# Attention and two mixture layers on one core: the third block's bias is begun later in the second block

## The chip, the core and the metric

The kernel runs on one core of a Trainium2 chip. The metric is the device time of one execution in microseconds (us); lower is better. The engines are TensorE (PE: matmuls; PEld: its weight loads), VectorE (DVE), ScalarE (ACT), GpSimd (POOL) and SyncE (SP, which here issues nearly all DMAs, in order).

## What is computed

Attention over 4 batches, 8 heads, 576 positions and head size 64, with a learned bias on relative position, and then two feed-forward layers over the 2304 rows:

```python
scores = scale * np.matmul(q, k.transpose(0, 1, 3, 2))
x = (psi_rel / psi_i)[..., None]            # log1p(|i-j|) / log1p(max(i,1))
bias = np.maximum(x @ w1 + b1, 0.0) @ w2    # 576 x 576 x 8 heads
attn = softmax(scores + bias)               # bias is the same for all batches
x = (attn @ v) as 2304 x 512
h = np.maximum(np.maximum(x @ w1, x @ w2), x @ w3)   # 512 -> 768
x = h @ w_out                                        # 768 -> 512
h = x @ w_in                                         # 512 -> 2048
x = g(h) @ w_out                                     # g: 0, a parabola, or h
```

## The kernel before

The 576 query positions are cut into five blocks: four of 128 and one of 64. The work on attention is a list of slots, each one head of one batch of one block: slots 0 to 31 are the first block, 32 to 63 the second, 64 to 95 the third, and then the fourth and the short fifth, interleaved. A slot has these steps:

- scores on TensorE (L692), made for two slots at a time into two PSUM buffers of the tile `s`;
- the softmax step on VectorE (L706): scores plus bias, and the row's extreme, which frees the buffer of `s`;
- the exponential (L708) and a cast to 16 bits (L724) on ScalarE, the residue of the cast on GpSimd (L725, a first part, and L726);
- a transpose by DMA on SP's queue (L728) into the tile `pt`;
- 14 value matmuls (L748), called for three slots later.

After the last slot of a batch the result is scaled (L760, VectorE), cast (L762) and its residue made (L763), and transposed by DMA into `xT` (L771).

Between these steps the kernel's slot loop puts other work:

- The bias of the next block, 18 groups for a block of 128. A group is a mask on VectorE (L390), 16 short matmuls on TensorE (L394), and a sum that every other group does on VectorE (L400, L401), the others on ScalarE and GpSimd (L403 to L406). The sum reads `xtab`, a table that is loaded from memory for each block (L298) and scaled on VectorE (L308); there is one buffer of it. Bias of two blocks is held at a time, in the two halves of `ab`; that of the short block lies in `ws` (L374 to L381, nine groups, its own table by L303).
- The first feed-forward layer for blocks that are done. Its first part is 12 matmuls of L803 for each of three weights, in one of three PSUM buffers of the tile `pm`. The first of a triple is emptied by ScalarE (L808), the others by VectorE (L810), and the maximum is cast (L814) and its residue made by GpSimd (L815). Its second part is 18 matmuls of L825, emptied by ScalarE (L830), reduced by VectorE (L831) and stored (L832).
- The split of the second part's weights into two 16-bit parts: six times L158 on ScalarE and L159 on VectorE, from slot 38 on.

How much of the bias a slot calls for is set by one list, a pair for each of the first three blocks: from which slot of the block on, and over how many slots. The loop adds a rate at every slot from the first number on, and calls for a group whenever the sum passes a whole number:

```python
b_at, b_n = PRM["bias"][min(u.j, 2)]
with sooner("bias"):
    for _ in range(rate("bias", (27 if u.j == 2 else 18) / b_n) if at >= b_at and not conv_left else 0):
        if bias_q:
```

The calls do not fix the final order. A scheduler orders the instructions of each engine by the priority of their calls (`sooner` lifts it) and by its own estimate of when inputs are ready. Each engine then runs its list in order.

Of the kernel before, what the change touches and what calls it, by code (L numbers as in the profile page):

```python
# [20 lines left out]
def kernel(ctx: ExitStack, tc: tile.TileContext, qt, kt, vr, small, mw1, mw2, mw3, mwo, win, wo2, out):  # L21
# [30 lines left out]
        peng='vv',  # L52
        warm=50,
        warm1=30,
        bias=[[12, 10], [6, 16], [3, 26]],
        c0=0.7,
        conv=[0.9, 0.36, 0.36, 0.36, 0.36],
        mlp=[2, 1.2, 1.5, 1.2, 1],
# [1193 lines left out]
```

## Time and profile before

| | |
|---|---|
| timed runs | median 1025.28 us of 3 (1022.13 to 1028.06) |
| profiled execution | 1021.94 us, its span 1020.2 us |
| TensorE busy | 937.5 us (92%) |
| VectorE, ScalarE, GpSimd busy | 716.9, 599.4, 512.1 us |
| mean granted clock of TensorE | 0.954 of full |

The span is the time between the first and the last instruction of the profiled execution. Busy times are sums over an engine's instructions; matmuls are pipelined, so a busy TensorE is not one at its peak. In the rows below, the number in square brackets behind an instruction is how long its engine stood idle before it and what ended that.

### The profile page before, as it was taken

How to read it: one execution, taken by the hardware profiler on the slowest of the kernel's cores; microseconds unless marked ns; L12 is line 12 of the kernel's file. 1: busy time of each engine (PE TensorE's matmuls, PEld its weight loads, DVE VectorE, ACT ScalarE, POOL GpSimd, SP SyncE). 2: the span in 40 equal slices, each digit the busy share in tenths (PEclk: the TensorE clock that was granted, in tenths of full speed). 3: DMA queues.
4: the chain of work that ended last, by engine and by line, in shares of the span. 5: the costliest groups of instructions: out<-in, count | busy, mean ns of one | idle time of the engine just before them, and what ended most of it. 6: DMA issues, size and time to landing. Idle time of an engine off the chain costs nothing. (4 is left out here: it accounts for less than half of the span.)

```text
span 1020.2 us, 26008 instructions
## 1 busy us (share of the span) xinstructions
PE 937.5 (92%) x10258; PEld 761.2 (75%) x10258; DVE 716.9 (70%) x1603; ACT 599.4 (59%) x1194; POOL 512.1 (50%) x734
## 2 busy tenths in 40 slices
PE   5768889899999989999999899979999999999996
PEld 5546678668888878777778778434588888888885
DVE  8897977796456677555454588798687686586565
ACT  3688875865556544769576689443344354444342
POOL 4132577676576754646357102886034344444452
PEclk7777879999999999999999999999999999999999
DMA  9897988999798988999999754010020010000000
GB/s 281 260 282 147 256 208 205 217 220 227 144 249 192 185 188 183 222 220 232 217 177 210 181 191 127 21 42 1 1 84 22 2 42 12 12 22 11 12 22 21
DMA packets 238970, 141.47 MB, mean 139 GB/s; under 512 B 187520, under 2 KB 217728, under 8 KB 238336
## 3 DMA queue, kind: packets, MB, share of 16 engines
q1 hardware_dynamic: 238688, 139.55, 58.5%
q8 instruction: 80, 1.31, 0.5%
q14 instruction: 42, 0.34, 0.1%
q10 hardware_dynamic: 160, 0.26, 0.1%
HBM read 79.68 MB, written 15.27 MB: 93 GB/s over the span
## 5 line engine op out<-in xcount | busy, mean ns | idle before, releaser
L803 PEld LDWEIGHTS <-aw 128*128 128x128 f16 x2160 | 190.6, 99 | 44.0 <-issue 22.0
L803 PE MATMUL pm<-xT,aw 128*128 128x256 f16 (+1 forms) x1812 | 203.9, 265 | 4.8 <-ACT hm L808 1.9
L726 POOL TENSOR_TENSOR phl<-sp,phl 128x512 f16<-128x512 f32 x136 | 160.9, 1183 | 0.0
L708 ACT ACTIVATE sp<-sp,mx 128x576 f32<-128x576 f32 x144 | 110.6, 768 | 77.6 <-DVE mx L706 77.2
L692 PE MATMUL s<-k,qz 64*128 64x288 f32 (+1 forms) x576 | 130.4, 464 | 11.6 <-DVE mx L706 9.0
L725 POOL TENSOR_TENSOR phl<-sp,phl 128x64 f16<-128x64 f32 x136 | 50.1, 368 | 176.0 <-ACT phl L724 143.0
L706 DVE CUSTOM_DVE_ANT_0 sp<-s,ab 128x576 f32<-128x576 f32 x128 | 93.2, 751 | 30.0 <-PE s L692 11.8
L1137 ACT ACTIVATE sp<-pm,vec 128x256 f32<-128x256 f32 x112 | 61.3, 556 | 85.9 <-PE pm L1120 84.6
L748 PEld LDWEIGHTS <-pt 128*128 128x128 f16 x1792 | 73.1, 101 | 30.2 <-DMA pt<-phl 20.1
L692 PEld LDWEIGHTS s<-k,qz 64*128 64x128 f32 (+1 forms) x576 | 70.8, 203 | 30.9 <-DVE mx L706 11.0
L724 ACT ACTIVATE phl<-sp 128x576 f16<-128x576 f32 x136 | 89.7, 673 | 3.6 <-DMA pt<-phl 3.0
L1141 POOL TENSOR_TENSOR hh<-hh 128x128 f32<-128x128 f32 x56 | 34.4, 614 | 107.9 <-DVE hh L1139 92.1
L748 PE MATMUL pav<-v,pt 128*128 128x64 f16 x1568 | 70.5, 196 | 14.6 <-DMA pt<-phl 14.5
L1120 PEld LDWEIGHTS <-ab 128*128 128x128 f16 x756 | 73.9, 98 | 9.4
L1138 DVE SCALAR_TENSOR_TENSOR hh<-pm,vec,sp 128x256 f32<-128x256 f32 x112 | 52.2, 477 | 33.5 <-ACT sp L1137 33.2
L825 PEld LDWEIGHTS <-wo 128*128 128x128 f16 x648 | 62.4, 99 | 15.9 <-issue 6.1
L825 PE MATMUL pm<-hh,wo 128*128 128x256 f16 x558 | 69.1, 276 | 3.6 <-ACT hh L814 1.4
L815 POOL TENSOR_TENSOR hh<-hm,hh 128x256 f16<-128x256 f32 (+1 forms) x60 | 44.0, 733 | 56.7 <-ACT hh L814 55.4
L1159 PEld LDWEIGHTS <-xT 128*128 128x128 f16 x588 | 57.5, 98 | 7.8 <-ACT xT L1146 1.2
L1159 PEld LDWEIGHTS <-wo 128*128 128x128 f16 x588 | 57.5, 98 | 6.7
L810 DVE SCALAR_TENSOR_TENSOR hm<-pm,hm 128x256 f32<-128x256 f32 (+1 forms) x108 | 41.9, 389 | 28.1 <-ACT hm L808 12.2
L1142 POOL TENSOR_TENSOR hh<-hh 128x128 f32<-128x128 f32 x56 | 26.5, 473 | 68.0 <-DVE hh L1139 61.0
(300 smaller groups left out, 2024.8 us busy)
## 6 DMA issues: line engine op xcount, KB each, us to landing
k<-in_k_dram SPq DMA_DIRECT2D x64, 288.0 KB, 4.0
v<-v_d SPq DMA_DIRECT2D x24, 640.0 KB, 4.9
ws<-in_moe_w_out_dram SPq DMA_DIRECT2D x15, 512.0 KB, 4.9
ws<-in_moe_w_in_dram SPq DMA_DIRECT2D x9, 512.0 KB, 5.1
x_d<-hl SPq DMA_DIRECT2D x36, 128.0 KB, 2.7
qz<-in_q_dram SPq DMA_DIRECT2D x16, 256.0 KB, 4.6
ab<-in_moe_w_dram SPq DMA_DIRECT2D x8, 512.0 KB, 9.3
qz<-x_d SPq DMA_DIRECT2D x4, 1024.0 KB, 4.7
```

The source lines that it names most:

```text
L692: last_score[0] = T.matmul(sbox[i + r][:, c, :288], q[p, s if u.j == SJ else s // 2], k[p, 288 * c:288 * c + 288], start=True, stop=True)
L706: last_pair[0] = V.tensor_tensor_reduce(halves(sn), sbox.pop(i)[:, :, :288], halves(bias_sb[u.j][:, h]), -0.125, 3e38, ALU.add, ALU.min, mx)
L708: last_soft[0] = A.activation(pf, sn, AF.Exp, scale=-1.0, bias=mx, accum_out=u.sums[:, h:h + 1])
L724: A.activation(hl[:, :S], pf, AF.Copy)
L726: G.tensor_tensor(hl[:, S + 64:], pf[:, :512], hl[:, :512], ALU.subtract)
L748: T.matmul(u.pav[:, 64 * h:64 * h + 64], pt[:, c], v[:, sl, 64 * (h % 4):64 * (h % 4) + 64], **kw)
L803: T.matmul(o, wm[:, ft, i, wp, kk], x_rhs(key, xp, kk) if n == 256 else x_rhs(key, xp, kk)[:, c], start=(x == 0), stop=(x == 11))
L825: T.matmul(pm, wo16[:, ft, wp, P * d:P * d + P], hh[:, ft, hp], start=(ft == 0 and y == 0), stop=(ft == NF1 - 1 and y == 2))
L1120: T.matmul(pm, w[:, wp, kk], x2t[ORDER[y]][:, kk, xp, 256 * sub:256 * sub + 256], start=(x == 0), stop=(x == 11))
L1137: A.activation(r, pm, AF.Relu, scale=c_ch[:, f], bias=c_half)
L1138: V.scalar_tensor_tensor(t, pm, c_c[:, f], r, ALU.mult, ALU.max)
L1159: T.matmul(m[x], gl[:, gp, i], w[:, wp], start=(start and z == 0 and x % 2 == 0), stop=(stop and z == 2 and (x % 2 == 1 or x == 6)))
```

## The change

The list's second pair is changed. The third block's bias is called for from the twelfth slot of the second block on (slot 44), not from the sixth (slot 38); the rate stays 18 groups in 16 slots.

```diff
         warm=50,
         warm1=30,
-        bias=[[12, 10], [6, 16], [3, 26]],
+        bias=[[12, 10], [12, 16], [3, 26]],
         c0=0.7,
```

The numbers of instructions stay as they are. The order of the engines differs between about slot 44 and slot 60, and in small ways between slots 84 and 92, where the short block's bias is built. On TensorE, before, the 18 runs of L394 stand between the scores of slots 44 and 58, after, between those of slots 46 and 60. Between the scores of slots 44 and 46 TensorE now has 72 matmuls of L803 where it had 36 and two runs of L394, and ahead of the value matmuls of slot 42 it has 60 of L803 and 18 of L825 more than before and one run of L394 less; the second part (L825) of the first layer's second unit begins ahead of the scores of slot 48, where it began behind those of slot 50. By the scores of slot 60 all has been done that had been done before.

VectorE, from slot 45 to slot 47; `wo` are the second part's weights, `ab` the bias, `hm` the first part's results. Before:

```order
L400 TENSOR_TENSOR btmp<-pm,xtab 128x256
L390 TENSOR_TENSOR masks<-rw,thr 128x1024
L401 SCALAR_TENSOR_TENSOR ab<-pm,vec,btmp 128x8x32
L810 SCALAR_TENSOR_TENSOR hm<-pm,hm 128x256
L159 SCALAR_TENSOR_TENSOR wo<-ws,vec,wo 128x512
L390 TENSOR_TENSOR masks<-rw,thr 128x1024
L159 SCALAR_TENSOR_TENSOR wo<-ws,vec,wo 128x512
L760 TENSOR_TENSOR xf<-pav,rd 128x512
L159 SCALAR_TENSOR_TENSOR wo<-ws,vec,wo 128x512 x2
L706 ISA sp,mx<-s,ab 128x576
```

And after, on VectorE at the same place:

```order
L810 SCALAR_TENSOR_TENSOR hm<-pm,hm 128x256
L159 SCALAR_TENSOR_TENSOR wo<-ws,vec,wo 128x512 x6
L760 TENSOR_TENSOR xf<-pav,rd 128x512
L810 SCALAR_TENSOR_TENSOR hm<-pm,hm 128x256 x2
L706 ISA sp,mx<-s,ab 128x576
L706 ISA mx 128x1
L706 ISA sp,mx<-s,ab 128x576
L706 ISA mx 128x1
L757 TENSOR_SCALAR rd<-sums 128x8
L758 RECIPROCAL rd<-rd 128x8
L810 SCALAR_TENSOR_TENSOR hm<-pm,hm 128x256 x2
```

The masks and sums of the bias have gone from among the six splits, two emptyings of the first part stand directly behind them, and the softmax steps of slots 46 and 47 follow each other.

ScalarE at the same place, after the change; `phl` are the 16-bit parts of a slot's exponentials, `hh` those of the first part's results:

```order
L158 ACTIVATE wo<-ws,vec 128x512 x6
L724 ACTIVATE phl<-sp 128x576
L814 ACTIVATE hh<-hm 128x256
L808 ACTIVATE hm<-pm 128x256
L762 ACTIVATE px<-xf 128x512
L814 ACTIVATE hh<-hm 128x256
L708 ACTIVATE sp,sums<-sp,mx 128x576 x2
L808 ACTIVATE hm<-pm 128x256
L724 ACTIVATE phl<-sp 128x576 x2
L814 ACTIVATE hh<-hm 128x256
```

Before, the two operations of the bias (L403, L404) stood behind the first cast here, and the exponentials of slots 46 and 47 were apart, with casts between them.

VectorE at the reload of `xtab` for the fourth block. Before, ahead of the softmax step of slot 58:

```order
L390 TENSOR_TENSOR masks<-rw,thr 128x1024
L810 SCALAR_TENSOR_TENSOR hm<-pm,hm 128x256
L308 TENSOR_SCALAR xtab<-xtab,vec 128x576
L810 SCALAR_TENSOR_TENSOR hm<-pm,hm 128x256
L706 ISA sp,mx<-s,ab 128x576
```

And after, on VectorE, where the steps around it are those of slots 60 and 61:

```order
L390 TENSOR_TENSOR masks<-rw,thr 128x1024
L760 TENSOR_TENSOR xf<-pav,rd 128x512
L706 ISA sp,mx<-s,ab 128x576
L706 ISA mx 128x1
L308 TENSOR_SCALAR xtab<-xtab,vec 128x576
L706 ISA sp,mx<-s,ab 128x576
L706 ISA mx 128x1
L810 SCALAR_TENSOR_TENSOR hm<-pm,hm 128x256 x2
```

The scaling of the reloaded table has moved from ahead of slot 58 to between the softmax steps of slots 60 and 61.

## Rows read from the trace of the kernel before

**Rows 1.** The page: TensorE's busy time, and the chain's shares by engine.

```profile
PE 937.5 (92%) x10258; PEld 761.2 (75%) x10258; DVE 716.9 (70%) x1603; ACT 599.4 (59%) x1194; POOL 512.1 (50%) x734
...
PE 30%; DVE 5%; DMA 3%; ACT 3%; POOL 2%; issue 1%; SPq 0%; POOLq 0%; ACTq 0%; DVEq 0%
```

**Rows 2.** Stretches: us from:to, length, busy us by engine (instructions), clock, DMA, GB/s.

```profile
210.00:220.00 10.00, 8.43 (x91) 6.42 (x92) 10.00 (x20) 5.51 (x12) 9.15 (x12) 0.83 1.16 212
200.00:270.00 70.00, 65.30 (x888) 53.45 (x886) 50.68 (x101) 39.91 (x95) 46.74 (x58) 0.98 0.98 204
270.00:360.00 90.00, 89.93 (x1265) 77.22 (x1263) 53.64 (x128) 55.20 (x136) 63.51 (x84) 1.00 0.99 203
```

**Rows 3.** Timeline of TensorE, 197 to 258 us: start, us, instruction, [idle before].

```profile
197.73 2.78 PE L803 MATMUL pm<-xT,aw 128*128 128x256 f16 x24
...
201.59 1.47 PE L803 MATMUL pm<-xT,aw 128*128 128x256 f16 x12 [0.53 <-ACT hm L808]
...
205.83 1.48 PE L803 MATMUL pm<-xT,aw 128*128 128x256 f16 x12
...
211.57 0.47 PE L748 MATMUL pav<-v,pt 128*128 128x64 f16 x10 [2.20 <-DMA pt<-phl]
211.88 2.58 PE L803 MATMUL pm<-xT,aw 128*128 128x256 f16 x12
...
214.60 1.65 PE L692 MATMUL s<-k,qz 64*128 64x288 f32 x4
...
216.69 1.24 PE L692 MATMUL s<-k,qz 64*128 64x288 f32 x4
...
235.02 2.14 PE L825 MATMUL pm<-hh,wo 128*128 128x256 f16 x18 [1.15 <-DVE ab L401]
...
243.18 0.98 PE L748 MATMUL pav<-v,pt 128*128 128x64 f16 x28
...
257.83 0.63 PE L394 MATMUL pm<-coef,masks 128*128 128x64 f16 x16
```

**Rows 4.** Timeline of VectorE, 206 to 266 us.

```profile
206.52 0.74 DVE L159 SCALAR_TENSOR_TENSOR wo<-ws,vec,wo 128x512 f16<-128x512 f32 x1
207.18 0.67 DVE L760 TENSOR_TENSOR xf<-pav,rd 128x512 f32<-128x512 f32 x1
207.78 2.40 DVE L159 SCALAR_TENSOR_TENSOR wo<-ws,vec,wo 128x512 f16<-128x512 f32 x2
210.11 0.74 DVE L706 CUSTOM_DVE_ANT_0 sp<-s,ab 128x576 f32<-128x576 f32 x1
...
214.57 0.74 DVE L706 CUSTOM_DVE_ANT_0 sp<-s,ab 128x576 f32<-128x576 f32 x1
...
265.68 0.52 DVE L308 TENSOR_SCALAR xtab<-xtab,vec 128x576 f32<-128x576 f32 x1 [4.71 <-DMA xtab<-log_d]
```

**Rows 5.** Timeline of ScalarE, 203 to 208 us.

```profile
203.35 3.77 ACT L158 ACTIVATE wo<-ws,vec 128x512 f16<-128x512 f32 x6
207.03 0.67 ACT L724 ACTIVATE phl<-sp 128x576 f16<-128x576 f32 x1
```

**Rows 6.** Timeline of GpSimd, 208 to 261 us.

```profile
208.03 1.60 POOL L726 TENSOR_TENSOR phl<-sp,phl 128x512 f16<-128x512 f32 x1
...
217.77 1.16 POOL L726 TENSOR_TENSOR phl<-sp,phl 128x512 f16<-128x512 f32 x1
...
260.42 0.72 POOL L405 TENSOR_TENSOR btmp<-btmp,xtab 128x256 f32<-128x256 f32 x1
```

**Rows 7.** Timeline of SP's queue, 261 us: the reload of xtab.

```profile
261.17 0.33 SPq L298 DMA_DIRECT2D xtab<-log_d  x1
```

**Rows 8.** Groups by line, 180 to 420 us: count | busy us, mean ns | idle before, releasers.

```profile
L708 ACT ACTIVATE sp<-sp,mx 128x576 f32<-128x576 f32 x65 | 49.9, 768 | 53.4 <-DVE mx L706 53.3
...
L810 DVE SCALAR_TENSOR_TENSOR hm<-pm,hm 128x256 f32<-128x256 f32 (+1 forms) x48 | 19.9, 414 | 14.8 <-ACT hm L808 7.8 <-PE pm L803 4.8 <-ACT phl L724 1.8
...
L159 DVE SCALAR_TENSOR_TENSOR wo<-ws,vec,wo 128x512 f16<-128x512 f32 x6 | 6.7, 1127 | 0.0
```

## The prediction

> **What bounds the kernel now.** The page comes first. TensorE is busy 937.5 of 1020.2 us, but the shares of the chain that ended last add up to 44% of the span (30 + 5 + 3 + 3 + 2 + 1) and stop there, so the chain says nothing on the stretch that the change touches [rows 1]. The question is where TensorE loses time between slot 44 and slot 60, and the table by stretches answers it [rows 2]. From 270 to 360 us TensorE is busy 89.93 of 90 us: it alone is the bound there. From 200 to 270 us it is busy 65.30 of 70, so 4.70 us are idle. Within that, from 210 to 220 us, the granted clock is 0.83 and VectorE is busy 10.00 of 10.00. Here the six second-layer weight splits (L158, L159), the third block's bias and the softmax steps (L706) meet. TensorE's rows are back in their old order by slot 60, at about 275 us. So the change can save what is lost between 200 and 275 us, and cost whatever new wait arises there.
>
> TensorE's own timeline shows the losses one by one [rows 3]: 0.53 us before 201.59, 2.20 us before 211.57 for a transposed softmax tile, 1.15 us before 235.02, and small ones. After the 2.20 us the clock is halved for a while: twelve L803 matmuls took 2.58 us at 211.88 against 1.48 at 205.83, and a pair's scores 1.65 at 214.60 against 1.24 at 216.69, so 1.10 + 0.41 = 1.5 us more. Idle and slow clock are 4.7 + 1.5 = 6.2 us.
>
> **What the change removes.** No instruction goes away: 18 groups of bias, each 16 short matmuls, are built before and after, and a run of 16 took 0.63 us [rows 3]. Only its neighbours change. VectorE no longer has masks and bias sums between the weight splits, so the softmax steps of slots 46 and 47, which began at 210.11 and 214.57 [rows 4], come back to back right after them. The tile that TensorE waited 2.20 us for is wanted later: 60 more L803 matmuls and 18 of L825 now stand ahead of it, and 12 of L803 take 1.30 us (24 took 2.78 us, 12 took 1.48), so 60 take 6.5. So the 2.20 us, the halved clock and most of the small waits lose their cause. I take all 6.2 us off, since each hangs on a neighbour that has moved. The lower bound is 2.2 us, the tile's wait alone.
>
> **What it adds: three waits, worked out along the new order.**
>
> A, behind the weight splits. ScalarE's six splits start at 203.35 and a cast of 0.67 us follows at 207.03 [rows 5]; then come two short operations of about 0.4 us each (L814, L808; L810, of their shape, has a mean of 0.414 [rows 8]). So a PSUM buffer is free at 207.03 + 0.67 + 0.8 = 208.5 us. TensorE has, from 200.5 us (197.73 + 2.78 [rows 3]), 48 L803 (5.2 us), 25 value matmuls (0.9, as 28 took 0.98) and scores (1.2), and arrives at 207.8: it waits 0.7. Its next two buffers stand behind all six L159 and L760. An L159 took 0.74 us at 206.52, while GpSimd had nothing in these rows, and two took 2.40 us at 207.78, while GpSimd ran one operation of 1.60 us from 208.03 [rows 4, 6]. From 204.0 us, when ScalarE's first split ends (203.35 plus a sixth of 3.77), I reckon two at 1.2 and four at 0.74, so to 209.3; L760 (0.67 [rows 4]) and L810 free the buffer at 210.4. TensorE is there at 208.5 + 1.3 + 0.15 = 209.95: 0.45 more. A is 1.1 us. Bounds: 0, and 2.6 if all six take their mean of 1.127 us [rows 8].
>
> The Trainium skill, SBUF — State Buffer, "SBUF: two separate sides", says that a VectorE instruction with two SBUF inputs and a GpSimd one that reads SBUF exclude each other for their whole length. By that rule one GpSimd operation of 1.16 us would stand fully between the splits, 204.0 + 6 x 0.74 + 1.16 = 209.6 us, and A would be 1.4.
>
> B, the last hidden tile. The last L803 triple before the second layer gets its low part from GpSimd (L815), now behind the residues of slots 46 and 47. The softmax steps start at 210.8 and end at 211.5 and 212.3 (0.74 each); exponentials of 0.77 us [rows 8] to 213.1, L808 to 213.5, two casts of 0.67 to 214.8. The residues take 1.16 us [rows 6] and some 0.3 for their first part, so they end at 215.7 and 217.2, and L815, at the 0.72 of a like GpSimd operation (L405 [rows 6]), at 217.9. TensorE runs two L803 groups to 213.0 and a few value matmuls to 213.2, waits 0.3 for the buffer that L808 frees, and with a bias run (0.5), 15 second-layer matmuls (1.6) and a second run is at the hidden tile at 216.3: it waits 1.6. B is 1.9 us, bounds 0 and 2.6 (a like error as in A).
>
> C, the reload of the table xtab. It may start when the last group of the third block's bias has read the old one. Before, the last run of L394 ended at 257.83 + 0.63 = 258.5, GpSimd's last read (L405) began at 260.42, the reload was issued at 261.17, and L308 began at 265.68 after 4.71 us of idle on VectorE [rows 3, 4, 6, 7]: 7.2 us from the run. TensorE had second-layer matmuls meanwhile. Now the last run lies 2.7 us before the end of the scores of slot 60 (9 L803, 14 value matmuls, scores: 1.0 + 0.5 + 1.2), and L308 stands between the softmax steps of slots 60 and 61. Step 61 ends 7.2 + 0.5 + 0.7 = 8.4 us after the run. TensorE has 2.7 + 3.6 = 6.3 us of work (24 L803 and 28 value matmuls more) before the next scores, which need that step's buffer: it waits 2.1. Bounds: 0, and 4.7, all of VectorE's old wait. I take 2.1, since both lengths come from rows.
>
> Queued behind these waits are the softmax steps on VectorE, the exponentials on ScalarE, the transposes on SP, and through them value matmuls three slots later, whose distance covers a short delay. SP also issues one weight load earlier, ahead of two transposes that are wanted those 6.5 us later: that I cost at nothing; without that cover it would be its place in the queue, half a microsecond.
>
> The second place, slots 84 to 92, has the same matmuls with the short block's bias slid by up to two slots. I take 0, bounds -1.2 and +1.2, one wait of the size of that at 235.02.
>
> **Sum.** -6.2 + 1.1 + 1.9 + 2.1 = -1.1 us. The profiled execution took 1021.94 us, so 1020.8; the three timed runs have a median of 1025.28, which is 1024.2 us on their scale.
>
> **Rivals.**
> 1. The added waits stay hidden: A and B go if the splits run at 0.74 us, C if the reload lands early. Then -6.2 us, 1019.1. For it: what is relieved is VectorE's full stretch. Against it: L308 already waited for its transfer [rows 4].
> 2. Nothing: bias is filler on TensorE, and the old waits return in full a few slots on, where bias and second layer now meet: 0, 1025.3. For it: 89.93 of 90 us busy right after. Against: the 2.20 us have a plain cause that goes.
> 3. The new waits halve the clock. The wait of 2.20 us was followed by that, the wait of 1.15 us was not [rows 3]. C is of the first size: 1.5 us, and as much again if A and B run together. Then -1.1 + 3.0 = +1.9, 1027.2. The Trainium skill, TensorE: Matmul & The Clock Gate, "HAM oscillation — how this bites in real kernels", states this cost for matmuls that keep waiting for transfers.
> 4. Slower: the reload of xtab stands in SP's queue behind the second layer's stores (L832). If it goes out late, L308 holds VectorE, and so every softmax step and PSUM emptying behind it; each us past the 7.2 is a us of TensorE. It decides from 5.1 + 1.1 = 6.2 us more, a reload that lands 13.4 us after the last run: 1030.4 and up. For it: the old wait of 4.71 us. Against: the stores ahead of it are not yet late in any row here.
>
> **How the numbers follow.** About 0.5% (5.1 us) is what timing this kernel can tell from no change. Chances: the forecast 0.45, rival 1 0.17, rival 2 0.15, rival 3 0.13, rival 4 0.10. Only rival 1 is faster by more than 0.5%, and only just: 0.16. Only rival 4 is slower: 0.10. The rest, 0.74, lies within. The range goes down to rival 1 at 1019.0 and up to where rival 4 begins, 1030.0, which leaves out rival 4 and the lower half of rival 1, under 2 in 10.
>
> **What would show it.** Right: no wait of 2 us for a transposed tile near slot 42 and full clock from 200 to 250 us; the steps of slots 46 and 47 back to back near 211 us; waits of TensorE near 208, near 217 and behind slot 60. Wrong: the same idle time from 200 to 275 us at other places (rival 2), a half-rate stretch after a new wait (rival 3), L308 waiting over 10 us (rival 4), or a difference that first arises past 400 us, where this sum has nothing.

## The result, and the profile after

The kernel after takes 1015.79 us (median of 6 runs, 1009.40 to 1017.13) against 1027.40 us for before in the same comparison (6 runs): ratio 0.9877, 95% interval 0.9847 to 0.9908. Two more comparisons of the same two programs, in the next section, gave 0.9926 (0.9892 to 0.9959) and 0.9934 (0.9905 to 0.9962). The change makes the kernel faster by 0.7 to 1.2%, 7 to 12 us; forecast were 1.1 us. A profile shows one execution, and executions of one kernel differ by about 1% (here by 7.73 us), so a profile can come from a fast or a slow one. The profiled execution took 1016.74 us, its span is 1014.9 us.

The page after: TensorE's busy time and the chain's shares. They answer to [rows 1] and tell as little: TensorE is busy 3.3 us less, and the chain is nearly the same.

```profile
PE 934.2 (92%) x10258; PEld 761.3 (75%) x10258; DVE 711.2 (70%) x1603; ACT 600.5 (59%) x1194; POOL 512.1 (50%) x734
...
PE 30%; DVE 5%; DMA 3%; ACT 3%; POOL 3%; issue 2%; SPq 0%; POOLq 0%; ACTq 0%; DVEq 0%
```

The stretches of after, as [rows 2]: us from:to, length, busy us by engine (instructions), clock, DMA, GB/s.

```profile
210.00:220.00 10.00, 7.86 (x133) 7.11 (x130) 2.78 (x10) 5.23 (x14) 6.23 (x9) 1.00 1.14 223
220.00:230.00 10.00, 8.82 (x110) 7.25 (x111) 6.58 (x16) 2.88 (x8) 1.94 (x2) 0.83 0.77 154
...
200.00:270.00 70.00, 66.20 (x945) 56.54 (x942) 47.23 (x103) 42.00 (x102) 48.70 (x61) 0.98 0.97 209
...
270.00:360.00 90.00, 89.64 (x1279) 76.85 (x1277) 56.03 (x131) 53.73 (x130) 66.15 (x88) 1.00 1.01 212
```

VectorE's full ten microseconds are gone (2.78 us busy from 210 to 220), but TensorE is still idle for 3.80 us between 200 and 270 us, where it was 4.70, and the granted clock still falls to 0.83 once, now from 220 to 230. So in this window the idle time that the forecast counted is only 0.90 us less. Most of the gain lies elsewhere, and fixed windows hide it, since the same work lies at other times in the two runs. The fair window runs from one score matmul to another: from the first of slot 42 to the first of slot 66, and of slot 80 to slot 100. Between these, TensorE does the same work in both (1197 rows of the trace in either for the first stretch, 959 and 960 for the second). In the two fences below, the first two rows are all of TensorE's work (with the other engines), the last two the score matmuls alone. First before, then after.

```profile
192.41:290.07 97.66, 92.01 (x1197) 75.64 (x1195) 65.44 (x145) 59.36 (x141) 62.61 (x81) 0.98 0.98 204
341.15:416.00 74.85, 72.02 (x959) 60.72 (x956) 52.95 (x132) 37.81 (x91) 44.58 (x61) 1.00 0.88 183
...
192.41:290.07 97.66, 20.49 (x96) 0.98 0.98 204
341.15:416.00 74.85, 15.80 (x80) 1.00 0.88 183
```

```profile
191.56:284.37 92.81, 88.35 (x1197) 74.83 (x1194) 60.27 (x145) 59.31 (x141) 62.41 (x81) 0.98 1.01 214
335.47:408.24 72.77, 71.05 (x960) 59.78 (x957) 53.11 (x132) 38.64 (x91) 44.41 (x61) 1.00 0.87 188
...
191.56:284.37 92.81, 16.81 (x96) 0.98 1.01 214
335.47:408.24 72.77, 15.60 (x81) 1.00 0.87 188
```

From slot 42 to 66 after is 4.85 us shorter. Only 1.19 of that is idle time (5.65 against 4.46); 3.68 us is TensorE busy for less time with the same 48 score matmuls (each is two rows, hence x96). From slot 80 to 100 it is 2.08 us shorter, 1.11 of it idle time. There TensorE waits in before for buffers that ScalarE empties (L830), where the short block's bias (L374) is built:

```profile
377.04 0.63 PE L374 MATMUL pm<-coefp,masks 128*128 128x64 f16 x16 [1.05 <-ACT hl L830]
...
381.36 0.63 PE L374 MATMUL pm<-coefp,masks 128*128 128x64 f16 x16 [0.96 <-ACT hl L830]
```

TensorE's timeline shows why the same matmuls took longer in before. A pair of slots has four score matmuls, x8 in the rows, two on rows 0 to 63 of the array and two on rows 64 to 127. Of before, the pairs of slots 46 (two rows) and 50 (three), and a whole one (slot 52):

```profile
204.19 1.23 PE L692 MATMUL s<-k,qz 64*128 64x288 f32 x6
...
207.23 0.75 PE L692 MATMUL s<-k,qz 64*128 64x288 f32 x2
...
220.62 0.76 PE L692 MATMUL s<-k,qz 64*128 64x288 f32 x4
...
221.82 0.75 PE L692 MATMUL s<-k,qz 64*128 64x288 f32 x2
...
225.79 0.75 PE L692 MATMUL s<-k,qz 64*128 64x288 f32 x2
...
238.25 1.24 PE L692 MATMUL s<-k,qz 64*128 64x288 f32 x8
```

The pair of slot 48 stands in [rows 3], as two halves of x4. Whole, a pair takes 1.24 us. In pieces (x6 + x2; x4 + x4; x4 + x2 + x2) the same four matmuls take 1.98, 2.89 (one half at halved clock) and 2.26 us. The pair of slot 58 is in three pieces too. In after only one pair of this stretch, that of slot 50, is in pieces.

TensorE's timeline of after, as [rows 3]: the start, the duration, and the idle time ahead of it.

```profile
206.97 1.47 PE L803 MATMUL pm<-xT,aw 128*128 128x256 f16 x12 [0.33 <-ACT hm L808]
...
215.78 2.13 PE L825 MATMUL pm<-hh,wo 128*128 128x256 f16 x18
...
220.96 1.00 PE L394 MATMUL pm<-coef,masks 128*128 128x64 f16 x16 [3.00 <-DVE masks L390]
...
222.29 3.17 PE L825 MATMUL pm<-hh,wo 128*128 128x256 f16 x18 [0.22 <-DVE ab L401]
...
233.41 0.75 PE L692 MATMUL s<-k,qz 64*128 64x288 f32 x2
...
234.67 1.23 PE L692 MATMUL s<-k,qz 64*128 64x288 f32 x6
```

VectorE's timeline of after, as [rows 4]:

```profile
202.74 4.81 DVE L159 SCALAR_TENSOR_TENSOR wo<-ws,vec,wo 128x512 f16<-128x512 f32 x6 [1.27 <-ACT wo L158]
...
208.86 0.75 DVE L706 CUSTOM_DVE_ANT_0 sp<-s,ab 128x576 f32<-128x576 f32 x1
...
209.53 0.75 DVE L706 CUSTOM_DVE_ANT_0 sp<-s,ab 128x576 f32<-128x576 f32 x1
...
219.94 0.37 DVE L308 TENSOR_SCALAR ws<-ws,vec 128x288 f32<-128x288 f32 x1 [6.06 <-DMA ws<-log_d]
...
272.25 0.52 DVE L308 TENSOR_SCALAR xtab<-xtab,vec 128x576 f32<-128x576 f32 x1 [1.18 <-DMA xtab<-log_d]
```

The softmax steps of slots 46 and 47 are back to back and the wait of 2.20 us for a transposed tile is gone. In its place is one of 3.00 us, which no step of the forecast names (a_again, a second profile of after, has only 0.83 us there): VectorE stands 6.06 us before it scales the *short* block's table (L308 on ws), masks for the third block's bias (L390) are queued behind it, and TensorE waits for these; the 18 L825 behind it took 3.17 us instead of 2.13. SP's queue of after shows why the table is late: its two loads are issued only at 213.81 us, behind two transposes that hold the queue for 5.81 us, one more transpose and two loads. VectorE comes to stand at that moment, so its 6.06 us are the time from the issue to the landing.

```profile
205.20 5.81 SPq L728 DMA_TRANSPOSE pt<-phl  x2
...
213.81 1.34 SPq L303 DMA_DIRECT2D ws<-log_d  x2
...
268.99 0.33 SPq L298 DMA_DIRECT2D xtab<-log_d  x1
```

The same wait stood in before, shorter, in VectorE's timeline; the wait of 1.15 us before 235.02 in [rows 3] is for a sum queued behind it:

```profile
232.94 0.37 DVE L308 TENSOR_SCALAR ws<-ws,vec 128x288 f32<-128x288 f32 x1 [3.44 <-DMA ws<-log_d]
```

### The profile page after: what moved, and what is told of

Same layout as the page of the kernel before. It is cut to its first block, busy times and chain, and to the rows that moved or that the text cites. A ratio compares the mean times of both kernels' runs of the same rounds, so it can differ in the third digit from the quotient of the medians.

```text
span 1014.9 us, 26005 instructions
## 1 busy us (share of the span) xinstructions
PE 934.2 (92%) x10258; PEld 761.3 (75%) x10258; DVE 711.2 (70%) x1603; ACT 600.5 (59%) x1194; POOL 512.1 (50%) x734
## 5 line engine op out<-in xcount | busy, mean ns | idle before, releaser
L803 PEld LDWEIGHTS <-aw 128*128 128x128 f16 x2160 | 192.0, 100 | 43.8 <-issue 21.7
L803 PE MATMUL pm<-xT,aw 128*128 128x256 f16 (+1 forms) x1812 | 204.8, 266 | 4.5 <-ACT hm L808 1.4
L726 POOL TENSOR_TENSOR phl<-sp,phl 128x512 f16<-128x512 f32 x136 | 161.2, 1185 | 0.0
L692 PE MATMUL s<-k,qz 64*128 64x288 f32 (+1 forms) x576 | 125.2, 456 | 12.6 <-DVE mx L706 10.2
L825 PEld LDWEIGHTS <-wo 128*128 128x128 f16 x648 | 61.7, 99 | 13.8 <-issue 6.2
L825 PE MATMUL pm<-hh,wo 128*128 128x256 f16 x558 | 70.2, 276 | 1.9 <-ACT hh L814 0.9
L810 DVE SCALAR_TENSOR_TENSOR hm<-pm,hm 128x256 f32<-128x256 f32 (+1 forms) x108 | 42.0, 390 | 27.9 <-ACT hm L808 10.2
```

Source lines behind the costliest of these rows:

```text
L692: last_score[0] = T.matmul(sbox[i + r][:, c, :288], q[p, s if u.j == SJ else s // 2], k[p, 288 * c:288 * c + 288], start=True, stop=True)
L726: G.tensor_tensor(hl[:, S + 64:], pf[:, :512], hl[:, :512], ALU.subtract)
L803: T.matmul(o, wm[:, ft, i, wp, kk], x_rhs(key, xp, kk) if n == 256 else x_rhs(key, xp, kk)[:, c], start=(x == 0), stop=(x == 11))
L825: T.matmul(pm, wo16[:, ft, wp, P * d:P * d + P], hh[:, ft, hp], start=(ft == 0 and y == 0), stop=(ft == NF1 - 1 and y == 2))
```

## The experiments

Two theories came out of this. **Pieces:** a pair of slots whose score matmuls are torn apart costs TensorE time, and the change pays because its order tears fewer. **Waits:** the pieces only fill time in which TensorE would wait anyway, and the change pays by the waits that it takes from VectorE. Every run was also timed against before on its chip. The interval of a ratio is some 0.3% to either side, as wide as most of what is to be told apart, so the stretches of the profiles decide, and the ratios say how much of it arrives. In profiles of these kernels, the first score of slot 42 comes at 187.4 to 199.5 us, though nothing ahead of it is changed: that is the scatter which the ratios have to average out.

| run | slots 42 to 66, us | idle | scores busy | slots 80 to 100, us | ratio to before (95%) | place |
|---|---|---|---|---|---|---|
| before | 97.66 | 5.65 | 20.49 | 74.85 | 1 | 1 of 4 |
| b_again (before again) | 98.09 | 7.39 | 20.08 | 74.60 | 0.9991 (0.9960 to 1.0022) | 4 of 12 |
| b_tab | 98.89 | 4.00 | 22.17 | 74.61 | 1.0014 (0.9981 to 1.0048) | 11 of 12 |
| b_whole | 97.91 | 9.36 | 16.64 | 73.55 | 0.9939 (0.9912 to 0.9967) | 11 of 12 |
| b_whole_2 | 97.58 | 7.28 | 16.63 | 73.64 | 0.9990 (0.9958 to 1.0022) | 6 of 12 |
| b_whole_tab | 93.38 | 5.15 | 16.63 | 73.88 | 0.9977 (0.9946 to 1.0007) | 6 of 12 |
| b_whole_tab_2 | 95.78 | 7.29 | 16.64 | 74.35 | 0.9915 (0.9880 to 0.9950) | 12 of 12 |
| after | 92.81 | 4.46 | 16.81 | 72.77 | 0.9877 (0.9847 to 0.9908) | 5 of 6 |
| a_again (after again) | 91.81 | 3.69 | 17.59 | 72.74 | 0.9926 (0.9892 to 0.9959) | 6 of 12 |
| a_again_2 | 92.70 | 4.59 | 16.81 | 72.72 | 0.9934 (0.9905 to 0.9962) | 2 of 12 |
| a_tab | 92.48 | 4.86 | 17.56 | 72.74 | 0.9895 (0.9863 to 0.9926) | 2 of 12 |
| a_slot3 | 97.10 | 6.15 | 17.57 | 73.34 | 0.9953 (0.9917 to 0.9990) | 9 of 10 |
| a_whole | 92.17 | 4.50 | 17.31 | 73.04 | 0.9942 (0.9908 to 0.9975) | 2 of 12 |
| a_whole_tab | 94.73 | 4.90 | 18.36 | 73.49 | 0.9970 (0.9940 to 1.0000) | 4 of 12 |
| a_apart | 96.16 | 6.00 | 18.79 | 80.15 | 1.0115 (1.0074 to 1.0156) | 1 of 4 |
| a_apart_46 | 95.27 | 5.04 | 18.55 | 72.84 | 0.9935 (0.9908 to 0.9963) | 12 of 12 |
| s15_whole | 91.01 | 4.20 | 16.63 | 71.83 | 0.9959 (0.9936 to 0.9982) | 2 of 12 |

Idle is the length less TensorE's busy time; the columns but the last two are rows of the view by stretches, as in the fences above. The place is that of the profiled execution among its kernel's executions by time, 1 the shortest. Names that begin with b start from before, with a from after. In kernels with edits, line numbers past the edit shift by a few.

**The two programs again.** b_again and a_again are before and after unchanged.

> The kernel before once more, for a second profile of it. Both theories: the same time, ratio 1.000 within 0.5%. Theory 1 (score pairs): TensorE's score rows of slots 46 to 51, 58 and 59 are again in more than four pieces, some 3.5 us longer in all than four whole pairs. Theory 2 (waits): the same 2 us wait for a transposed tile near 211 us and half clock after it. If the timed median of before (1027.4) lies above its first profile (1021.94) for a reason inside slots 44 to 60, this profile shows that stretch longer than 88.2 us (slot 45 to slot 64); if for a reason elsewhere, the stretch is again 88 us.

> The changed kernel once more, for a second profile. Ratio to before 0.985 to 0.991 as measured. Slot 45 to slot 64 takes 83.4 us as in the first profile if the gain there is fixed by the order, and the rest of the difference of the medians lies in other stretches.

> The kernel after once more. The two comparisons so far gave 0.988 and 0.993. By the profiles the stretches from slot 42 to 66 and from 80 to 100 are 7 to 8 us shorter than in before, and the others differ from run to run only: ratio 0.992 to 0.993, 91.5 to 93 us from slot 42 to 66 and 72.8 from 80 to 100.

The gain is there each time. In TensorE's timeline of b_again the wait for the transposed tile is there again, but the halved clock behind it is not (granted 1.00 from slot 42 to 66), and the stretch is no shorter for it:

```profile
212.71 0.47 PE L748 MATMUL pav<-v,pt 128*128 128x64 f16 x10 [2.21 <-DMA pt<-phl]
```

By the table's rows, two profiles of before have a mean of 97.88 us from slot 42 to 66, three of after 92.44: 5.44 us less, of which the scores make 3.2 (20.29 to 17.07) and idle time 2.3 (6.52 to 4.25). From slot 80 to 100 it is 74.73 to 72.74, 2.0 us. Together 7.4 us, 0.7% of the time, which two of the three ratios give; the rest of the first ratio is scatter of the other stretches.

**Order inside a pair.** a_slot3 emits the third block's pairs slot by slot instead of alternating between the two halves of the rows:

```
+            if u.j == 2:
+                cr = [(c, r, p) for r, p in enumerate(rows) for c in range(2)]
```

> The changed kernel, but the scores of a pair in the third block (slots 64 to 95) are made slot after slot, not with the two slots' matmuls in turn; no work more or less. Theory 1 (two slots' score matmuls use different row halves and run side by side, so that a pair made in pieces costs more): a pair takes 2.3 us, not 1.17, 1.17 us more for each of 16 pairs, of which at least the ten of slots 64 to 83 lie where TensorE is the bound: 12 to 19 us slower than the changed kernel, ratio to before near 1.00 to 1.01. Theory 2 (only waits count, matmuls cost the same in any order): the time of the changed kernel within 2 us, ratio 0.988.

The expectation of a price fell: TensorE's timeline of a_slot3 has such a pair, still in one piece, at 1.25 us.

```profile
287.83 1.25 PE L694 MATMUL s<-k,qz 64*128 64x288 f32 x8
```

So the order in which a pair's matmuls are emitted costs nothing, as long as they stay together. Whether separation does was left open by this run. Its stretch from slot 42 to 66 is out of line, 97.10 us: that execution has place 9 of 10, the wait behind the short block's table was followed by a long stretch of halved clock (18 matmuls of L825's kind took 3.53 us, clock 0.96 in the stretch), and the scores behind the reload of xtab waited 1.23 us more. One profile is a sample, and this is how far it can lie off.

**Pairs torn apart on purpose.** a_apart emits each slot of the third block by itself, so that other matmuls stand between the two slots of a pair:

```
+            alone = u.j == 2
+            if alone:
+                ...
+                p = slice(64 * (s % 2), 64 * (s % 2) + 64)
+                for c in range(2):
+                    last_score[0] = T.matmul(sbox[i][:, c, :288], q[p, s // 2], k[p, 288 * c:288 * c + 288], start=True, stop=True)
+                return
```

> The kernel after with the third block's scores (slots 64 to 95) emitted one slot at a time, two matmuls each on their own 64 rows, so that other matmuls stand between the two slots of a pair. The number of matmuls is the same. Theory: two matmuls on the same rows take 1.16 us, so a pair takes 2.3 us instead of 1.17 in a stretch in which TensorE is never idle: 16 pairs, +17 us, ratio about 1.009 to before. Rival (the longer score time is only how the trace models ends; pieces cost nothing): within 1.5 us of after.

Two slots of one pair in TensorE's timeline, and the stretch from slot 66 to 80 of a_apart (length, TensorE busy):

```profile
301.94 1.23 PE L692 MATMUL s<-k,qz 64*128 64x288 f32 x4
...
306.71 1.24 PE L692 MATMUL s<-k,qz 64*128 64x288 f32 x4
...
285.97:345.67 59.70, 59.70 (x740) 1.00 0.87 167
```

The same stretch of after:

```profile
284.37:335.47 51.10, 51.02 (x740) 1.00 1.00 216
```

Half a pair alone takes as long as a whole one. Seven pairs, 8.60 us more, 1.23 us a pair, and the run is slower by 1.0115 - 0.9926 = 1.9%, 19 us. This is the theory of pieces where TensorE is never idle: in these runs two matmuls on different halves of the rows ran beside one another only where no other matmul stood between them in the queue. The Trainium skill, TensorEngine Tiling (Array Packing), "Key Properties", says that tiles of the array can execute matmuls in parallel; the trace agrees (x8 in 1.24 us, x4 on one half in 1.23). A further piece has a price of its own, but a small one: a pair in two pieces that each hold both halves, as in after at slots 88 to 92, takes 0.69 us for each piece from its start to the next row's, 1.38 in all, against 1.17 for a whole pair. Of the first stretch the edit reaches only the last pair, slot 64's.

**Pairs held together in before.** b_whole is to keep the four matmuls of each pair of slots 42 to 95 together, with the bias at its old place (in the trace the pair of slot 44 is in two halves, those from slot 46 to 66 are whole): the matmul whose buffer comes free last goes first, the other three follow at once.

```
-                for r, p in enumerate(rows):
+                for r, p in (reversed(list(enumerate(rows))) if hold else enumerate(rows)):
+                    down = min(2000, tc.cur_priority) if hold and prev else 0
+                    tc.cur_priority -= down
+                    with tc.issue_after(prev.ins) if prev and hold else nullcontext():
                     ...
+                    tc.cur_priority += down
+                    prev = prev or last_score[0]
```

> The kernel before, with the four score matmuls of each pair of slots 42 to 95 held together in TensorE's order (the slot whose buffer comes free last goes first, the other three follow at once), bias as before. Theory (score pairs in pieces cost TensorE time of their own): the pairs of slots 46, 48, 50, 58 and 92 take 1.2 to 1.4 us each instead of 1.85 to 2.75, so TensorE's time on scores from slot 42 to 66 falls from 19.4 to about 15.5 us, and the run is 3.5 to 5 us faster than before: ratio 0.995 to 0.9965. Rival (a pair is made in pieces only because its second buffer is late, and TensorE has nothing else to do anyway): the score time falls just as much, the idle time rises by as much, and the run is within 0.15% of before.

> The kernel before with pairs held together once more, for a second profile, since the first run's times were 0.6% under before and its profile from slot 42 to 66 was not. If the 3.94 us wait for the short block's table came from its transfer that time (6.4 us), the transfer takes 3.5 to 4.5 us now and the stretch 94 to 96 us. If it comes from the order, the wait is again 3.5 us or more and the stretch 97.5 us or more.

The scores take 3.5 to 3.9 us less, and the stretch is as long as ever (97.91, 97.58): idle time took it. That is the theory of waits, and in VectorE's and TensorE's timelines of b_whole one wait stands out:

```profile
231.87 0.37 DVE L308 TENSOR_SCALAR ws<-ws,vec 128x288 f32<-128x288 f32 x1 [5.63 <-DMA ws<-log_d]
```

```profile
232.63 1.01 PE L394 MATMUL pm<-coef,masks 128*128 128x64 f16 x16 [3.94 <-DVE hm L817]
```

It is the short block's table again. In b_whole_2 the wait is 3.60 us on VectorE and 2.10 on TensorE, with the loads again late (5.6 us from issue to landing, 3.5 in before), so it came with this order both times and was not one late transfer, which the second expectation had supposed possible. The second place gains 1.1 to 1.2 us in the two runs, 0.84 of it in the scores, above all in the pair of slot 92. The ratios, 0.9939 and 0.9990, do not say more than that a little arrives; the profile of the first has place 11 of 12.

**The table's wait alone, and both together.** b_tab and a_tab scale the short block's table only behind a softmax step of the third block:

```
+                with tc.issue_after(last_pair[0].ins) if j == SJ else nullcontext():
                     xscale(j, xts[j])
```

> The kernel before with one edit: the scaling of the short block's table (L308 on ws), for which VectorE stood 3.4 us at 232.9 us, is issued only behind a softmax step of the third block, long after its transfer has landed. Pairs in pieces stay. Theory (the wait on that table costs TensorE something in both kernels, 1.1 us of idle time in before): slots 42 to 66 take 96 to 97 us instead of 97.7 to 98.1, ratio to before 0.998. Rival (VectorE has room there, the wait costs nothing): 97.7 or more, ratio 1.000.

> The changed kernel, but the scaling of the short block's table (L308 on ws) stands about 38 slots later on VectorE, behind slot 85's softmax step, not behind slot 47's. If the wait of 3.0 us on TensorE at 221 us and the half clock after it hang on VectorE's 6.06 us wait for that table, they go: 4 to 5 us faster than the changed kernel. Rival: the bias group behind it waits for something else as well (stores, buffers), and TensorE's idle time only moves: within 1 us.

> The kernel before with pairs held together and the scaling of the short block's table moved behind the third block's steps. With pairs held together alone, TensorE's scores took 3.5 us less from slot 42 to 66, and a wait of 3.94 us for that table (its transfer took 6.4 us that time, against 3.5 in before) gave it back. Theory: without the table's wait the gain shows, 93 to 94.5 us from slot 42 to 66, and as much as after is faster: ratio 0.991 to 0.993 with the second place. Rival (VectorE's rush between slots 45 and 50 bounds the stretch whatever the scores take): 96.5 us or more, ratio 0.996 or more.

> The kernel before with pairs held together and the short block's table scaled later, once more. One profile had 93.4 us from slot 42 to 66, where each edit alone had 97.6 to 98.9. Theory (two causes that hide one another): 93 to 94.5 us again, ratio 0.993 to 0.996. Rival (chance of one execution): 96.5 us or more.

Alone, the edit shortens the stretch in neither kernel: 98.89 against 97.88 us on average in before (idle 2.5 us less, but the clock was 0.95 and the torn pairs took 22.17 us), 92.48 against 92.44 in after. The profile of b_tab has place 11 of 12 and says little by itself; its ratio leaves room for a gain of 2 us at most. Together with whole pairs it brings before from 97.88 to 93.38 us. The second such profile has 95.78; that execution has place 12 of 12 and 7.3 us idle, so it neither confirms the first nor gives the old value back. The ratios don't decide it: 0.9977 and 0.9915 with both edits, 0.9939 and 0.9990 with whole pairs alone. As far as one profile can show it, before has two causes that hide one another: torn pairs and the table's wait. After is rid of most of the first, and of the rush on VectorE, by its order.

> The kernel after with the same holding together of pairs. Left there to mend are the pairs of slots 50 (1.85 us) and 88 to 92 (1.38 to 1.45 each), 1.2 us in all against 1.17 for a whole pair. Theory: 1 to 1.5 us faster than after, ratio to before about 0.991. Rival: as after, about 0.9925.

> The kernel after with both edits. Slots 42 to 66 took 91.8 to 92.8 us in after with or without either edit alone. Theory: each removes a wait that the other leaves, 90 to 91 us, ratio to before 0.988 to 0.990. Rival (with bias later that stretch is bound by TensorE's work itself, some 88 us, plus waits that only change place): 92 us, ratio as after, 0.992.

In after there is nothing left to mend by these edits: 92.17 us with whole pairs, much as without the edit. With both it got worse, 94.73, by a wait that the forecast had as term C: the reload of xtab came late, L308 stood 5.02 us on VectorE, and the next scores 2.97, at halved clock besides. TensorE's timeline of a_whole_tab:

```profile
271.59 2.96 PE L697 MATMUL s<-k,qz 64*128 64x288 f32 x8 [2.97 <-DVE mx L713]
```

**Pieces put back into after.** a_apart_46 emits slots 46 to 49, 58 and 59 one at a time (the edit of a_apart, with that list in place of the third block); in TensorE's order two pairs are then torn, and that of slot 50 is whole.

> The kernel after with the scores of slots 46 to 49, 58 and 59 emitted one slot at a time. In TensorE's order two pairs (48, 58) are then in two pieces of two matmuls on the same rows each, 2.33 us a pair instead of 1.17. Theory (in after, nothing hides such pieces): 2.0 to 2.5 us more from slot 42 to 66 than in after, 94 to 95 us; the later stretches as in after. Rival (there is room in that stretch): 91.8 to 92.8 us, with less idle time by as much as the scores take more.

95.27 us, 2.5 to 3.5 more than the three profiles of after, with no less idle time (5.04 us). Of the 2.8 us more than their mean, 1.5 are scores (18.55 against 17.07). So in this execution the torn pairs weren't hidden by idle time, but it has place 12 of 12, and the ratio, 0.9935, is that of after on the same chip (a_again_2, 0.9934). So the timed runs do not show that torn pairs cost time in after; their interval is as wide as the cost.

**Later still.** s15_whole begins the bias at slot 15 (`[15, 16]`), with pairs held together.

> The third block's bias begun at slot 15 of the second block (later again by three slots), with pairs held together. TensorE's order has then no pair in pieces past slot 45. If the gain goes with the pieces and with the stretch of VectorE's rush around slot 46, it is the same as for after with whole pairs, ratio 0.990 to 0.992; if bias later still collides with the second layer's work of slots 59 on, idle time there rises and the ratio goes back to 0.995 or more.

It has the shortest stretch to slot 66, 91.01 us, and pays behind it: from slot 66 to 80 it takes 55.09 us where after takes 51.10, 3.45 of it idle. The third block's bias is complete by then (its last run of L394 begins at 274.75 us, the scores of slot 66 at 283.57). The idle time is the wait that the forecast had as term C: SP issues the reload of xtab behind two transposes that hold its queue for 7.03 us, and L308 starts 13.7 us after the last run of L394 has ended. VectorE stands 6.25 us for it, and TensorE 2.03 and 1.42 us for buffers that VectorE empties behind it (here L817 is the L810 of before, and L810 its L803):

```profile
283.57:338.66 55.09, 51.64 (x755) 1.00 0.99 196
...
289.07 0.52 DVE L308 TENSOR_SCALAR xtab<-xtab,vec 128x576 f32<-128x576 f32 x1 [6.25 <-DMA xtab<-log_d]
...
289.98 0.27 PE L810 MATMUL pm<-xT,aw 128*128 128x256 f16 x1 [2.03 <-DVE hm L817]
...
291.67 0.63 PE L394 MATMUL pm<-coef,masks 128*128 128x64 f16 x16 [1.42 <-DVE hm L817]
```

No version is shown to be better than after; a_tab's ratio is lower by 0.3% than that of a_again on the same chip, within both intervals.

## Why the prediction was wrong, point by point

- **What the kernel loses from slot 42 to 60: the step that failed.** The sum took TensorE's work as the same wherever it stands, and counted only idle time and halved clock, 6.2 us. By the rows, about 3.2 of the 5.4 us gained from slot 42 to 66 are score pairs no longer torn, a term that the sum had at nothing. The sign stood in [rows 3]: the scores at 214.60 and 216.69, which the forecast calls a pair's, are x4, each half a pair, and the second took 1.24 us at full clock, the time of a whole one. I compared the two with one another for the clock and did not ask why half a pair takes so long. Rival 1 names the nearest time (-6.2 us) for another reason.
- **"I take all 6.2 us off": too much.** The 2.20 us went, and so did the halved clock behind it; the 1.5 us of that clock were no fixed loss of before, as b_again shows. The cause of the 1.15 us did not go. That wait hung on the short block's table, and in after the same table made one of 3.00 us (220.96; 0.83 in a_again), with a stretch of halved clock of its own. Idle time fell by 2.3 us on average, net of all that was added.
- **A, 1.1 us: measured 0.33** (206.97). The six splits took 4.81 us in a row; I had two at 1.2 us, and measured are one at 1.45 and five at 0.74 to 0.79. The first stood beside a GpSimd operation of 1.16 us (L726, from 202.48). The Trainium skill, SBUF — State Buffer, "SBUF: two separate sides", says that two such operations exclude each other; the trace agrees for this split, which took 0.71 us more than the next. A did not come to the 1.4 us worked out from that rule.
- **B, 1.9 us: measured 0.** TensorE has no wait between 207.3 and 217.9 us.
- **C, 2.1 us: measured 0 in after**, where L308 waited 1.18 us and the scores none. The mechanism is real: TensorE waited 0.84 us in a_tab, 2.97 in a_whole_tab, 3.45 in s15_whole. It hangs on how late the reload lands. From the end of the last run of L394 to L308 it was 4.7 us in after, 6.0 in a_tab, 7.8 in a_whole_tab and 13.7 in s15_whole; the forecast took over the 7.2 us of before. In s15_whole the reload is as late as rival 4 has it (13.4).
- **Steps 46 and 47 back to back, no 2 us wait for a transposed tile: right** (208.86, 209.53). "Near 211" was 2 us late, with A's splits.
- **The second place, taken as 0: measured -2.0 us.** In before TensorE waited 1.05 us at 377.04 and 0.96 us at 381.36 for buffers that ScalarE empties (L830); in after, where the short block's bias stands elsewhere, these waits are gone and others of 0.85 us and less have come. Idle time is 1.0 us less on average. The pair of slot 92, in three pieces in before, is in two in after, as are those of slots 88 and 90, so the scores gain only 0.2 us. The rest is other busy time; why it fell was not looked into, and no run tests this place.
- **The halved clock as rival 3 has it** came once, behind the 3.00 us, and cost 1.04 us on 18 L825 (in a_again it did not come).

So three waits were over-sized by 4.8 us, one was missed, and too much was taken off. These errors nearly cancelled, which is luck: idle time and clock together were forecast at -1.1 us from slot 42 to 66, and idle time fell by 2.3. What the sum lacked altogether are 3.2 us of TensorE's busy time in torn pairs and the 2.0 us of the second place. What stays open: how the 5.4 us divide between torn pairs and waits, since whole pairs alone did not shorten the stretch in before (b_whole, b_whole_2) and that torn pairs and the table's wait hide each other rests on one profile (b_whole_tab); and the scatter of the stretches that no edit touches (12 us up to slot 42, 6 us behind slot 100).

## What to carry to other kernels

An engine's busy time is not a constant of the work: compare the same instructions between two marks of the program, not between two times, and look at the count in a row as well as at its duration. Matmuls that use half of the array's rows should be issued next to their partner; an order that puts filler between them pays for it with up to the whole duration (1.23 us a pair in a_apart), unless TensorE would have waited there. Where one edit does nothing, a second cause may stand right behind it: try the two together before dropping either.

## What the runs showed of the hardware that was not expected

Two matmuls of 288 f32 columns on the same 64 rows took 1.23 us (x4), and so did four on both halves (x8, 1.24); one alone took 0.75 and two on different halves 0.76 (x2, x4). The order in which such a group was emitted made no difference (1.25 us). Each of the two loads of 72 KB that make up the short block's table was 3.4 to 6.4 us from issue to landing in these runs (median of the two, by run), and the instruction waiting for them held everything behind it on VectorE (6.06 us in after). A wait of TensorE of 2.20 us was followed by halved clock in before, one of 2.21 us in b_again was not.
